# Moving the last two products of two layers behind the next layer's first product, with a matmul prelude on zeros and two conversions moved to DVE, in an attention and two-layer-pair kernel on one Trainium2 core

## The chip, the cores and the metric

The kernel runs on one core of one Trainium2 chip. The metric is device time in microseconds (us); a kernel is run several times and the median is given. The engines are PE (TensorE, matmuls), DVE (VectorE), ACT (ScalarE), POOL (GpSimd, here mostly an issuer of DMAs) and SP (SyncE, an issuer of DMAs). PSUM is the memory into which PE writes; here it is four tiles, ps0 to ps3, of two banks each, and a bank holds 448 columns of float32 results.

## The reference

Attention with a sigmoid in place of the softmax, then two pairs of dense layers; everything is float32:

```python
scores = (1 / 8) * q @ k.T - log(448)          # q, k, v: 4 batches, 12 heads, 448 x 64
x = sigmoid(scores) @ v                        # x: 1792 tokens x 768
h = x @ w_in;  g = h - tanh(h);  y = g @ w_out             # 768 -> 2048 -> 768
h = y @ w_in2; g = max(h, 0) + alpha * min(h, 0)           # 768 -> 2048
out = g @ w_out2                                           # 2048 -> 768
```

## The kernel before, in words

**Numbers.** A float32 operand is split into a high and a low float16 half. The high half is one scaled copy (ACT or DVE can do it), the low half is one instruction on DVE, which needs the high one. A product is three passes on PE (high by high, high by low, low by high; `PASSES`).

**Attention.** `scores` multiplies a pair of heads (`st0` to `st23`, the split of the loads `sqk0` to `sqk23`) into ps0, ps1 or ps2 in turn, ACT takes the sigmoid out of it, and `values` multiplies that by v into ps3. A ps tile is free for the next scores when its sigmoid is done. The first pair is loaded in two halves; every split is a node that either ACT or DVE may take ("AV").

**Layers.** The four dense layers are counted 0 to 3 in the code, and 0 and 2 are the wide ones (`layer_in`), 1 and 3 the narrow ones (`second_layer`, `fourth_layer`, both through `multiply_out`). Each layer multiplies 2 x 2 blocks with seven products instead of eight, in the order `SEQ` = 1, 2, 6, 5, 7, 4, 3; sums of blocks are formed on DVE or by accumulating DMAs. The tokens come in two halves (sb = 0, 1). In layers 0 and 2 each product of each quarter q is a node of 18 matmuls into a whole ps tile: products 1, 6, 7, 4 of a quarter go into ps0 or ps1 (by q % 2), 2 into ps2, 5 and 3 into ps3. After product 7 of a quarter ACT copies the tile out; product 4 then writes into the same tile. To hide that copy, products 4 and 3 of a quarter (`tail`) are emitted after products 1 and 2 of the next quarter. For the last quarter there is no next one, and they come right after product 7.

In layers 1 and 3 a product is twelve groups of six matmuls (four quarters of the contraction by three rows of blocks e = 0, 1, 2); a group takes one bank. Products 1, 6, 7, 4 accumulate in the three banks `YB`, products 2, 5, 3 in the three banks `ZB`. When the last quarter of product 1, 6, 7 or 4 is done, ACT reads the three `YB` banks (`copied`); `added` on DVE reads the `ZB` banks. Products 7 and 4 are neighbours and both write into `YB`.

**Order.** Nothing is issued in the order of the code. Every step is a node of `Plan` with costs and due times; PE's nodes keep the order in which they are added, and for ACT, DVE, POOL and SP the planner runs a clock of its own and takes whichever ready node is due first, so far as its tables (`AHEAD`, `CHAIN`, `KEEP_*`, `WIN_*`, `PACE`) let it. So the tables set what stands in each engine's queue, and an engine works its queue strictly in order. The planner keeps one entry for each bank; the tile framework underneath puts in the semaphore waits. The weights are put together from two words by DVE, split, stored to a scratch in device memory by POOL's DMAs and fetched back by SP's.

All instructions are recorded through one helper, so each has line L213 in the profile, and rows are told apart by operation, tile and time.

## Time and profile before

| | |
|---|---|
| median of 3 runs | 904.79 us (904.16 to 906.05) |
| the profiled execution's own time | 904.37 us |
| span in that profile, first to last instruction | 902.6 us |
| PE, DVE, ACT busy share of the span | 99%, 88%, 71% |
| granted TensorE clock over the span | 1.000 |

The profiled execution took 1.8 us more than its span. Times in rows count from the start of the span. Attention fills PE until 130 us; layer 0 then runs to 323, layer 1 to 515, layer 2 to 707 and layer 3 to 898. PE's busy time has modelled ends, so a busy PE can hide short stalls between matmuls.

### The profile page before, as it was taken

How to read it: one execution, taken by the hardware profiler on the slowest of the kernel's cores; microseconds unless marked ns; L12 is line 12 of the kernel's file. 1: busy time of each engine (PE TensorE's matmuls, PEld its weight loads, DVE VectorE, ACT ScalarE, POOL GpSimd, SP SyncE). 2: the span in 40 equal slices, each digit the busy share in tenths (PEclk: the TensorE clock that was granted, in tenths of full speed). 3: DMA queues.
4: the chain of work that ended last, by engine and by line, in shares of the span. 5: the costliest groups of instructions: out<-in, count | busy, mean ns of one | idle time of the engine just before them, and what ended most of it. 6: DMA issues, size and time to landing. Idle time of an engine off the chain costs nothing.

```text
span 902.6 us, 13531 instructions
## 1 busy us (share of the span) xinstructions
PE 889.6 (99%) x4992; PEld 436.9 (48%) x4992; DVE 794.3 (88%) x1002; ACT 637.6 (71%) x879; POOL 156.4 (17%) x243
## 2 busy tenths in 40 slices
PE   7999999999999999999999999999999999999998
PEld 2333335555555455555455555555555455555554
DVE  6999999999999999999999999999987998684310
ACT  7999998999999787998575766756564655332310
POOL 0122523341222110100123142112110000000000
PEclk9999999999999999999999999999999999999999
DMA  9999999999978975655599999679872445453431
GB/s 352 371 351 333 278 383 401 280 233 270 275 248 254 288 222 167 223 185 202 175 324 348 340 297 382 209 239 362 291 250 88 140 159 193 141 191 120 138 136 62
DMA packets 67490, 223.46 MB, mean 248 GB/s; under 512 B 8416, under 2 KB 14816, under 8 KB 67424
## 3 DMA queue, kind: packets, MB, share of 16 engines
q0 software_dynamic: 25664, 109.33, 38.3%
q1 hardware_dynamic: 41760, 113.27, 36.2%
q8 instruction: 39, 0.64, 0.3%
q14 instruction: 27, 0.22, 0.1%
HBM read 154.94 MB, written 49.55 MB: 227 GB/s over the span
## 4 chain that ended last, share of the span: by engine, by line
PE 87%; DVE 8%; ACT 2%; issue 2%; DMA 1%; POOL 0%; SPq 0%; DVEq 0%; ACTq 0%
PE ps L213 87%; DVE slot L213 8%; ACT slot L213 2%; DMA slot<-qk 1%; DVE sc L213 0%; POOL sc L213 0%; SPq L213 0%; POOL scr L213 0%; DVEq L213 0%; ACTq L213 0%
## 5 line engine op out<-in xcount | busy, mean ns | idle before, releaser
L213 PE MATMUL ps<-slot,slot 128*128 128x448 f16 (+2 forms) x4416 | 836.5, 370 | 4.1 <-ACT slot L213 2.4
L213 PEld LDWEIGHTS <-slot 128*128 128x128 f16 (+1 forms) x4608 | 416.8, 98 | 422.6 <-issue 32.8
L213 ACT ACTIVATE slot<-slot 128x896 f32<-128x896 f32 (+3 forms) x288 | 250.9, 903 | 72.6 <-DVE slot L213 54.9
L213 ACT ACTIVATE slot<-slot,sc 128x896 f16<-128x896 f32 (+2 forms) x170 | 169.9, 1020 | 95.7 <-PE ps L213 43.2
L213 DVE SCALAR_TENSOR_TENSOR slot<-slot,sc,slot 128x896 f16<-128x896 f32 (+1 forms) x160 | 174.9, 1115 | 34.6 <-ACT slot L213 34.4
L213 DVE TENSOR_TENSOR slot<-slot,slot 128x896 f32<-128x896 f32 (+2 forms) x178 | 177.2, 1018 | 0.2
L213 DVE SCALAR_TENSOR_TENSOR slot<-slot,slot 128x768 f16<-128x768 f32 (+2 forms) x137 | 131.4, 970 | 8.4 <-ACT slot L213 8.2
L213 POOL DMA_DIRECT2D scr<-slot x112 | 67.8, 605 | 352.8 <-DVE slot L213 318.8
L213 DVE SCALAR_TENSOR_TENSOR slot<-stage,slot 128x768 int32<-128x768 int32 x128 | 120.3, 955 | 0.2
L213 ACT ACTIVATE slot<-ps 128x448 f32<-128x448 f32 (+1 forms) x88 | 60.6, 709 | 32.9 <-PE ps L213 32.4
L213 ACT ACTIVATE slot<-ps,cst 128x896 f32<-128x896 f32 x84 | 80.2, 1027 | 2.1 <-PE ps L213 2.0
L213 DVE SCALAR_TENSOR_TENSOR slot<-ps,sc,slot 128x896 f32<-128x896 f32 (+1 forms) x42 | 39.5, 950 | 44.1 <-PE ps L213 31.3
L213 ACT ACTIVATE slot<-ps,sc 128x896 f32<-128x896 f32 (+1 forms) x56 | 46.8, 838 | 38.4 <-PE ps L213 38.2
L213 POOL DMA_DIRECT2D stage<-w x60 | 36.1, 602 | 181.3 <-DVE slot L213 152.9
L213 POOL DMA_DIRECT2D slot<-slot x56 | 52.2, 1018 | 61.0 <-DVE slot L213 33.2
L213 PE MATMUL ps<-slot 64*128 64x448 f16 (+1 forms) x576 | 57.6, 362 | 4.9 <-ACT slot L213 4.9
L213 DVE TENSOR_SCALAR slot<-stage 128x768 int32<-128x768 int32 x64 | 35.3, 557 | 6.8 <-PE ps L213 6.6
L213 PEld LDWEIGHTS ps<-slot,slot 128*64 128x64 f32 (+1 forms) x384 | 20.1, 135 | 38.6 <-issue 37.5
L213 DVE COPY_PREDICATED slot<-slot,slot 128x896 f32<-128x896 int32 x32 | 38.3, 1216 | 0.0
L213 DVE TENSOR_SCALAR slot<-slot 128x768 f16<-128x768 f32 (+2 forms) x50 | 28.9, 590 | 0.4 <-DMA slot<-qk 0.3
L213 ACT ACTIVATE junk<-slot 128x448 f16<-128x448 f32 (+1 forms) x36 | 25.4, 705 | 3.3 <-DVE slot L213 2.8
L213 DVE TENSOR_TENSOR slot<-ps,slot 128x896 f32<-128x896 f32 (+1 forms) x28 | 24.6, 889 | 2.2 <-ACT slot L213 1.3
(28 smaller groups left out, 141.9 us busy)
## 6 DMA issues: line engine op xcount, KB each, us to landing
slot<-scr SPq DMA_DIRECT2D x224, 384.0 KB, 4.6
stage<-w POOLq DMA_DIRECT2D x60, 768.0 KB, 7.4
scr<-slot POOLq DMA_DIRECT2D x112, 384.0 KB, 6.1
slot<-slot POOLq DMA_DIRECT2D x32, 384.0 KB, 7.0
slot<-qk SPq DMA_DIRECT2D x23, 448.0 KB, 7.9
slot<-v SPq DMA_DIRECT2D x12, 448.0 KB, 7.5
slot<-slot POOLq DMA_DIRECT2D x24, 224.0 KB, 7.9
out_t<-slot SPq DMA_DIRECT2D x24, 224.0 KB, 2.0
```

What stands on the lines that cost most here:

```text
L213: return lambda *args, **kw: self.tc.keep_in_program_order(f(*args, **kw))
```

## The change

The last two products of layers 0 and 2 are no longer emitted at the end of `layer_in` but handed to the next layer, which emits them behind its first product (sb = 0). For this the banks of layers 1 and 3 are dealt out anew: `YB` was one bank of each of ps0, ps1 and ps2 and is now both banks of ps0 and one of ps2; `ZB` was both banks of ps3 and one of ps2 and is now both banks of ps1 and one of ps2. DVE sets `junk` to zero and PE multiplies it nine times into ps3 before anything else. The high halves of `st1` and `st2` may go to DVE alone. The planner's tables get other numbers (two lines are shown), the costs of the attention nodes are a little lower, and the first six loads are taken to land a microsecond later.

```diff
-CHAIN = {0: 7, 1: 3, 2: 5, 3: 7}
+CHAIN = {0: 2, 1: 3, 2: 6, 3: 7}
...
-KEEP_W, KEEP_F, KEEP_P, WIN_F, WIN_O, WIN_P, SPARE_V, WIN_Q = 7, 5, 12, 14, 43, 29, 8, 16
+KEEP_W, KEEP_F, KEEP_P, WIN_F, WIN_O, WIN_P, SPARE_V, WIN_Q = 8, 8, 1, 14, 29, 8, 12, 24
+WARM = 9
...
-        add("AV", {"A": act(n, ptr=ptr), "V": vec(n, ptr, True)}, high, [*reads, *extra],
+        add(on, {"A": act(n, ptr=ptr), "V": vec(n, ptr, True)}, high, [*reads, *extra],
...
-                  (j,) if halves == 2 else (0, 1))
+                  (j,) if halves == 2 else (0, 1), on="V" if i in (1, 2) else "AV")
...
-    YB = ((0, 0), (1, 0), (2, 0))
-    ZB = ((3, 0), (3, 1), (2, 1))
+    YB = ((0, 0), (0, 1), (2, 0))
+    ZB = ((1, 0), (1, 1), (2, 1))
...
-    def multiply_out(m, sb, P, copied, added):
+    def multiply_out(m, sb, P, copied, added, between):
...
+            if pr == 1:
+                for each in between:
+                    each()
...
+    V.memset(junk, 0.0)
+    for _ in range(WARM):
+        PE.matmul(pst[3][:, 0, 0:S], junk[:, 0:128], junk[:, 0:S], start=True, stop=True)
...
                 tail = [fourth, third]
-        for each in tail:
-            each()
+        return tail
...
-    layer_in(0, copy_h, finish_h, last_h, ended_h)
+    tail = layer_in(0, copy_h, finish_h, last_h, ended_h)
     for sb in range(2):
-        second_layer(sb)
+        second_layer(sb, () if sb else tail)
```

Layers 2 and 3 are changed in the same way.

**Three places in the order of the instructions.** The first is DVE's queue from its first instruction, before; slot0 to slot7 hold the loads there, and the results are the splits of `st0` to `st4`.

```order
L213 SCALAR_TENSOR_TENSOR slot8_183<-slot0_175,slot8_183 128x448 [waits DMAHW0_49,Activation_49]
L213 SCALAR_TENSOR_TENSOR slot8_183<-slot0_175,slot8_183 128x448 [waits DMAHW1_49,Activation_49]
L213 SCALAR_TENSOR_TENSOR slot0_175<-slot1_176,slot0_175 128x896 [waits DMAHW2_49,DVE_49,Activation_49]
L213 TENSOR_SCALAR slot11_186<-slot2_177 128x896 [waits DMAHW3_49]
L213 SCALAR_TENSOR_TENSOR slot11_186<-slot2_177,slot11_186 128x896 [waits DVE_49]
```

And after the change (the helper's line is now L214):

```order
L214 MEMSET junk_235 128x448
L214 SCALAR_TENSOR_TENSOR slot10_185<-slot0_175,slot10_185 128x448 [waits DMAHW0_49,Activation_49]
L214 SCALAR_TENSOR_TENSOR slot10_185<-slot0_175,slot10_185 128x448 [waits DMAHW1_49,Activation_49]
L214 TENSOR_SCALAR slot11_186<-slot1_176 128x896 [waits DMAHW2_49]
L214 SCALAR_TENSOR_TENSOR slot11_186<-slot1_176,slot11_186 128x896 [waits DVE_49]
```

The memset is new and stands first. The high half of `st1` (TENSOR_SCALAR out of slot1) is now on DVE; before, ACT made it, and DVE's third instruction waited for ACT. In ACT's queue the sigmoids now follow the two half-width copies of `st0` directly.

The second place is PE's queue at the end of layer 0 (slot41, slot43 and slot47 are operands and weights). Before, product 7 of the last quarter, into ps1, is followed by product 4, into ps1 again:

```order
L213 LDWEIGHTS slot43_218
L213 MATMUL ps1_237<-slot41_216,slot43_218 128x448
L213 LDWEIGHTS slot47_222 [waits DMAHW0_49]
L213 MATMUL ps1_237<-slot29_204,slot47_222 128x448 [waits Activation_49]
L213 LDWEIGHTS slot47_222
```

After the change, product 7 is followed by layer 1's first group, into ps0:

```order
L214 LDWEIGHTS slot50_225
L214 MATMUL ps1_237<-slot5_180,slot50_225 128x448
L214 LDWEIGHTS slot47_222 [waits DMAHW0_49]
L214 MATMUL ps0_236<-slot3_178,slot47_222 128x448
L214 LDWEIGHTS slot47_222
```

The wait for ACT is gone there; product 4 into ps1, with its wait for ACT's copy, comes 72 matmuls later, and product 3 behind it.

The third place is ACT's queue in layer 1, sb = 0, around the copies after product 7. Before (the copies are the rows out of ps0, ps1 and ps2):

```order
L213 ACTIVATE slot34_209,mx_233<-slot44_219,sc_234 128x896 [waits DVE_49]
L213 ACTIVATE slot12_187<-ps0_236 128x448 [waits PE_49]
L213 ACTIVATE slot33_208<-ps1_237 128x448 [waits PE_49]
L213 ACTIVATE slot34_209<-slot47_222,cst_232 128x896 [waits Activation_49]
L213 ACTIVATE slot18_193<-ps2_238 128x448 [waits DMAHW5_49,PE_49]
```

After the change:

```order
L214 ACTIVATE slot14_189<-ps0_236 128x448 [waits DMAHW4_49,PE_49]
L214 ACTIVATE slot20_195<-slot18_193 128x896 [waits DVE_49]
L214 ACTIVATE slot12_187,mx_233<-slot1_176,sc_234 128x896 [waits DVE_49]
L214 ACTIVATE slot21_196,mx_233<-slot24_199,sc_234 128x896 [waits DVE_49]
L214 ACTIVATE slot12_187<-ps0_236 128x448 [waits PE_49,Activation_49]
L214 ACTIVATE slot16_191<-ps2_238 128x448 [waits DVE_49]
```

The first two copies now read two banks of one tile, ps0, and three activations of 896 columns stand between them, each of which waits for DVE.

## Rows read from the trace of the kernel before

**Rows 1.** PE's waits by releaser: us in total, times, longest us.

```profile
PE ps L213 <- ACT slot L213: 7.4, 5, 4.6
PE ps L213 <- DVE slot L213: 1.3, 2, 0.7
```

**Rows 2.** Stretches: length, busy time of PE, PEld, DVE, ACT, POOL, clock, DMA share.

```profile
20.00:130.00 110.00, 110.00 (x858) 36.94 (x856) 108.23 (x151) 107.78 (x144) 32.73 (x49) 1.00 0.98 341
130.00:320.00 190.00, 188.58 (x1002) 97.25 (x995) 186.96 (x234) 177.59 (x227) 52.42 (x75) 1.00 0.92 286
390.00:515.00 125.00, 124.21 (x657) 64.07 (x655) 123.69 (x158) 89.07 (x138) 25.24 (x38) 1.00 0.79 259
```

**Rows 3.** PE's timeline at the begin: start, length, count, idle before and its releaser.

```profile
5.35 2.44 PE L213 MATMUL ps<-slot 64*128 64x448 f16 x12
...
8.32 2.54 PE L213 MATMUL ps<-slot 64*128 64x448 f16 x18 [0.15 <-ACT slot L213]
11.02 0.76 PE L213 MATMUL ps<-slot 64*64 64x448 f16 x12 [0.15 <-ACT slot L213]
...
13.37 1.31 PE L213 MATMUL ps<-slot 64*128 64x448 f16 x12
```

**Rows 4.** ACT's timeline at the begin.

```profile
6.42 0.95 ACT L213 ACTIVATE slot<-slot 128x896 f16<-128x896 f32 x1 [1.85 <-DMA slot<-qk]
7.28 6.38 ACT L213 ACTIVATE slot<-ps,cst 128x896 f32<-128x896 f32 x7
```

**Rows 5.** DVE's timeline at the begin.

```profile
7.41 1.09 DVE L213 SCALAR_TENSOR_TENSOR slot<-slot,slot 128x896 f16<-128x896 f32 x1 [2.18 <-ACT slot L213]
8.42 0.62 DVE L213 TENSOR_SCALAR slot<-slot 128x896 f16<-128x896 f32 x1
```

**Rows 6.** PE's timeline, the four longest idle times after the begin.

```profile
315.95 2.24 PE L213 MATMUL ps<-slot,slot 128*128 128x448 f16 x11 [1.42 <-ACT slot L213]
...
354.33 1.86 PE L213 MATMUL ps<-slot,slot 128*128 128x448 f16 x9 [0.57 <-DVE slot L213]
...
449.25 2.05 PE L213 MATMUL ps<-slot,slot 128*128 128x448 f16 x10 [0.74 <-DVE slot L213]
...
700.32 1.86 PE L213 MATMUL ps<-slot,slot 128*128 128x448 f16 x9 [1.01 <-ACT slot L213]
```

**Rows 7.** ACT's timeline at the end of layer 0.

```profile
314.91 0.99 ACT L213 ACTIVATE slot<-ps,sc 128x896 f32<-128x896 f32 x1
```

**Rows 8.** DVE's timeline before two of those idle times end.

```profile
353.13 3.27 DVE L213 SCALAR_TENSOR_TENSOR slot<-slot,sc,slot 128x896 f16<-128x896 f32 x3
...
448.04 1.15 DVE L213 TENSOR_TENSOR slot<-ps,slot 128x448 f32<-128x448 f32 x2
```

**Rows 9.** ACT's timeline around the copies after product 7, layer 1, sb = 0.

```profile
390.46 0.94 ACT L213 ACTIVATE slot<-ps 128x448 f32<-128x448 f32 x2
391.31 1.03 ACT L213 ACTIVATE slot<-slot,cst 128x896 f32<-128x896 f32 x1
392.24 0.52 ACT L213 ACTIVATE slot<-ps 128x448 f32<-128x448 f32 x1
```

**Rows 10.** ACT's timeline before the same copies for sb = 1: two splits.

```profile
481.78 1.56 ACT L213 ACTIVATE slot<-slot 128x768 f16<-128x768 f32 x2
```

**Rows 11.** ACT's timeline around the same copies in layer 3, sb = 0.

```profile
773.43 0.63 ACT L213 ACTIVATE slot<-ps,sc 128x448 f32<-128x448 f32 x1 [6.98 <-PE ps L213]
773.96 1.03 ACT L213 ACTIVATE slot<-slot,sc 128x896 f16<-128x896 f32 x1
```

**Rows 12.** The page, part 5: groups with count, busy us, mean ns of one.

```profile
L213 PE MATMUL ps<-slot,slot 128*128 128x448 f16 (+2 forms) x4416 | 836.5, 370 | 4.1 <-ACT slot L213 2.4
...
L213 DVE COPY_PREDICATED slot<-slot,slot 128x896 f32<-128x896 int32 x32 | 38.3, 1216 | 0.0
```

**Rows 13.** The timeline's last rows of PE and DVE.

```profile
893.66 4.89 PE L213 MATMUL ps<-slot,slot 128*128 128x448 f16 x25
897.46 1.89 DVE L213 SCALAR_TENSOR_TENSOR slot<-ps,sc,slot 128x448 f32<-128x448 f32 x3 [24.75 <-PE ps L213]
```

24 lines of the change are left out of this document (12 added, 12 removed).

## The prediction

> **What bounds the kernel now.** I read the busy shares of the table first: PE 99% of the span, DVE 88%, ACT 71%. So a gain can only come out of PE's few stalls and out of the time before its queue is dense. PE's waits come to 7.4 us on ACT, 4.6 of it ahead of the first matmul, and 1.3 on DVE; none is put down to a DMA [rows 1]. The stretches say how much room the others have: from 20 to 130 us DVE is busy 108.23 and ACT 107.78 of 110, from 130 to 320 DVE 186.96 of 190, from 390 to 515 DVE 123.69 of 125 [rows 2]. PE is the bound, but DVE stands right behind it until layer 2; whatever lets PE run ahead by more than a few us there meets DVE.
>
> PE's timeline then shows where it stops. After the begin there are four stalls above 0.5 us: 1.42 and 1.01, released by ACT, and 0.57 and 0.74, released by DVE [rows 6]. The first two are the ends of layers 0 and 2: product 4 waits for ACT's copy of the tile that product 7 has just left. At the end of layer 0 that copy began at 314.91 and took 0.99 [rows 7].
>
> At the begin, twelve matmuls from 5.35 take 2.44 us, while twelve of the same shape from 13.37 take 1.31 [rows 3]. They run in pairs: six pairs at 0.37 apart against 0.19. 448 columns take 0.373 us at 1.2 GHz and 0.187 at 2.4, so the first scores ran at the lower of the clock's two levels, although the granted-clock column reads 1.00 everywhere [rows 2]. But what holds PE there is ACT: it idles 1.85 us for the second load, makes the high half of `st1` from 6.42 to 7.37, and only then begins seven sigmoids back to back at 7.28 [rows 4]; PE waits for a sigmoid at 8.32 and 11.02 [rows 3]. From 11.02 on its queue is dense.
>
> **The start.** The memset (448 columns; an estimate is no more than the 0.62 that DVE takes for 896 [rows 5]) and the nine matmuls (9 x 0.37 = 3.4 us at the lower level) fit before the first real matmul at 4.6 [rows 1]. The first score's third pair starts at 5.35 and ends 0.58 later even at the lower level, by 5.95 [rows 3], so the first sigmoid can begin 1.3 us earlier once the high half of `st1` is off ACT. At the higher level it could be 1.6 earlier; but on DVE that high half takes 0.62 from 6.42 (a TENSOR_SCALAR of this shape) and the low one 1.09 [rows 4, 5], to 8.15; the fourth score, with two pairs behind that and 0.35 for the last, ends about 8.75, when the fourth sigmoid is due (5.95 + 3 x 0.91 = 8.7). So the start gives **1.3** with either clock; range 0.8 to 1.6, since DVE gets 1.24 of work in a stretch in which it also has idle time [rows 5].
>
> **The tails.** Product 7 is now followed by layer 1's first product into ps0 and ps2, which PE left four products (some 13 us) or more earlier. The copies have 12 groups, 13.6 us, to finish. This takes away **1.42 + 1.01** [rows 6]. The new neighbour, product 2 into ps1 behind product 3, needs ps1 read out while product 3 runs (18 x 0.189 = 3.4 us [rows 12]): one copy of 0.99 in layer 0, two reads of that size in layer 2 [rows 7], which fit, so I cost it at nothing; were ACT 1 us late, that would be the price. The scales and splits of sb = 1 come 13.6 us later, but are due some 90 us later; DVE turns to weights meanwhile. In SP's queue the fetches of the two moved products change places with the four of layer 1's first product; PE waited for no fetch before [rows 1], so I cost that at nothing too.
>
> **DVE's stalls.** The 0.57 at 354 is a low half that DVE reaches too late, one of three in a row [rows 8]. In the new order about five instructions of some 1 us fewer stand ahead of it on DVE, so the stall goes, although PE comes 2.7 us (1.3 + 1.42) earlier. For the fourth quarter of that product there is only about one fewer; I put **0.3** (0 to 1.8) there, since DVE also has less idle time at the begin. The 0.74 at 449 is of another kind: PE wants bank 0 of ps2, and what ends the stall is DVE's second read from 448.04, out of bank 1 [rows 6, 8]. A wait is by tile, not by bank. The last rows say so again: the last three groups end at 898.55, 897.41 and 896.28 (1.135 each), and DVE, idle for 24.75, reads the first of them, in ps3, only at 897.46, when ps3's other bank is done too [rows 13]. In the new order that read of ps2 is emitted behind PE's group, the wait falls three groups later, and the **0.74** goes.
>
> **The price of pairing the banks.** This is what the new `YB` costs. Products 7 and 4 both write `YB`, and two of its banks are now one tile. With ps0, ps1, ps2 the copy of bank e had two groups' time, 2.27 us, before product 4 needed it. Now copy 0 cannot begin before group 1 of product 7 ends. Count from that end: product 4's first group is due at 0.97 (one group less the 0.17 by which a matmul's end overlaps the next [rows 12]), its second at 2.11. Four such places:
> - Layer 3, twice: copies of 0.53 apart and 0.63 long [rows 11], 0.05 to start, 0.06 to pass on: 1.27, so **0.3** each (0 to 0.8).
> - Layer 1, sb = 1: a weight split of 0.78 [rows 10] stands between the copies in the new order: 0.05 + 0.45 + 0.78 + 0.54 + 0.06 = 1.88, so **0.9** (0.3 to 1.5).
> - Layer 1, sb = 0: three activations of 896 columns at 0.93 stand between them (third place in the order): 0.05 + 0.45 + 2.79 + 0.52 + 0.06 = 3.87, against 2.11: 1.76. Two of the three wait for a predicated copy of 1.22 on a full DVE [rows 12], so I take **2.2**; between 0.6 (copy 1 has only to wait for product 4's first group) and 3.5 (both predicated copies late).
>
> Before, ACT had the first two in 0.94 [rows 9] and PE did not stop there.
>
> The Trainium skill speaks for the other result. "PSUM — Partial Sum Buffer", section "PSUM bank collisions raise a hardware error", says that engines collide by bank and quadrant of partitions, and advises to guard by bank; by that rule two banks of one tile need no wait, the four places would cost nothing, and the net gain would be 5.04 - 0.3 = 4.7 us. By the rows the wait is there all the same, put in by tile: the rule bears on what the chip needs, not on the waits that this program has.
>
> **The sum.** Gains 1.3 + 1.42 + 1.01 + 0.57 + 0.74 = 5.04. Losses 0.3 + 0.3 + 0.3 + 0.9 + 2.2 = 4.0. Net 1.0 us: 904.37 - 1.0 = 903.3 for an execution like the profiled one (its span and the 1.8 around it, which I leave as they are). The median of the runs lies 0.42 above that execution, so I forecast **903.7**. A measurement of this kernel can tell about 0.2% from no change, which is 1.8 us; this forecast is inside.
>
> **Rivals.**
> - *The pairing is cheap* (0.33). ACT and DVE are ahead of PE at the four places and the copies cost only what they must: 0.6 + 0.3 + 0 + 0, and the net gain is 5.04 - 0.3 - 0.9 = 3.8: 904.8 - 3.8 = 901.0. For it: ACT is busy only 89 of 125 us from 390 on [rows 2]. Against it: the three activations stand in the queue between the copies, and an engine does not pass them. The skill's rule above, were the waits by bank, would end here too.
> - *The paired copies are late by ACT and DVE both: slower* (0.12). The place is the same four passages. The copy after product 7 already began late in layer 1 before, at 390.46 [rows 9]. If such a delay of 1 us meets each passage, and the three activations wait for DVE in full, the four cost 3.5 + 1.9 + 2 x 1.3 = 8.0 instead of 3.7, and the time is 908.0. It decides, that is passes 906.6, from 6.6 us of stalls there on.
> - *The early gains are not kept* (0.07). ACT and DVE are 98% busy from 20 to 130 [rows 2]; if they cannot run 1.3 us earlier, or DVE cannot follow PE in layer 1 (the 0.57 stays, the fourth quarter costs 1.8), the gain comes back as stalls: 903.7 + 1.3 = 905.0 without the start, 903.7 + 0.57 + 1.5 = 905.8 with DVE late in layer 1.
> - *The forecast* (0.48): 903.7, own range 902.4 to 905.2; about a tenth of it lies below 903.
>
> The range that should hold 8 in 10 reaches from the cheap pairing, with 0.4 for a begin that gives 1.6, to the early gains lost with a little of the late copies: 900.6 to 906.2. Faster by over 0.2% (below 903.0): 0.33 and 0.05 of the forecast's own, 0.38. Slower by over 0.2% (above 906.6): 0.12. Within: 0.50.
>
> **What would show it.** Right: the seven sigmoids from about 6.0; no stall at the ends of layers 0 and 2; in layer 1, a PE stall near 2 us about 386 us (product 4's second group, released by ACT) and one near 0.9 about 485; 0.3 twice in layer 3, all before groups into ps0. Wrong: PE passing these places without a stall, or stalls released by DVE or a DMA anywhere in layers 1 to 3 that together pass 2 us; PE stalling on ACT within attention; or sigmoids that still begin after 7 us.

## The result

The changed kernel is **slower**: 909.90 us median of six runs (908.53 to 912.83) against 905.42 (904.16 to 906.72) for the kernel before; ratio 1.0051, 95% interval 1.0037 to 1.0065. That is 4.5 us more, where 1.7 less was forecast, and outside the range of the forecast. The profiled execution took 908.66 us with a span of 906.9, against 904.37 and 902.6, so the two profiles differ by the 4.3 us that are to be explained. Of the changed kernel's six runs the two with a mean granted clock of 1.000 took 908.53 and 908.66 (the profiled one) and the four with 0.998 or 0.996 took 909.58 to 912.83, so its median also holds time at the lower clock, of which its profile shows nothing.

I begin with PE's milestones, found by counting matmuls in both timelines; the last column says how far the changed kernel is behind.

| PE begins | before | after | behind |
|---|---|---|---|
| the seventh scores (twelve 64x64 matmuls) | 11.02 | 11.64 | 0.62 |
| layer 0 | 130.48 | 132.07 | 1.59 |
| layer 1, sb = 0, product 2 | 336.37 | 336.38 | 0.01 |
| the same, product 6, fourth quarter | 360.94 | 361.83 | 0.89 |
| layer 1, sb = 1 | 418.83 | 422.34 | 3.51 |
| layer 2 | 515.28 | 519.35 | 4.07 |
| the last matmul's end | 898.55 | 902.48 | 3.93 |

So between these two profiles the start lost where it should have gained (how much of that is a load that landed later stands under "The begin" below); the moved products gave back all of that at the end of layer 0; and layer 1 lost more than 3 us after that. PE's waits of the changed kernel, by releaser (us in total, times, longest), and the group of layer matmuls on its page, whose last numbers are the idle time ahead of them, answer to [rows 1, 12]:

```profile
PE ps L214 <- ACT slot L214: 5.2, 6, 2.0
PE ps L214 <- DVE slot L214: 3.0, 5, 1.5
PE ps L214 <- DVE junk L214: 1.4, 1, 1.4
```

```profile
L214 PE MATMUL ps<-slot,slot 128*128 128x448 f16 (+2 forms) x4416 | 837.2, 370 | 6.6 <-ACT slot L214 4.3 <-DVE slot L214 2.0
```

The idle time ahead of that group rose from 4.1 to 6.6. Here 0.89 of it stands in attention and 5.65 in the four layers (before 4.0). PE's timeline, the longer of these stalls, each the idle time at the row's end (compare [rows 6]):

```profile
33.88 1.72 PE L214 MATMUL ps<-slot,slot 128*64 128x448 f32 x8 [0.89 <-ACT slot L214]
...
353.89 40.00 PE L214 MATMUL ps<-slot,slot 128*128 128x448 f16 x210 [1.45 <-DVE slot L214]
395.85 14.92 PE L214 MATMUL ps<-slot,slot 128*128 128x448 f16 x78 [1.96 <-ACT slot L214]
410.99 9.24 PE L214 MATMUL ps<-slot,slot 128*128 128x448 f16 x48 [0.23 <-ACT slot L214]
...
491.38 19.46 PE L214 MATMUL ps<-slot,slot 128*128 128x448 f16 x102 [0.66 <-ACT slot L214]
511.41 2.81 PE L214 MATMUL ps<-slot,slot 128*128 128x448 f16 x14 [0.57 <-ACT slot L214]
...
781.29 3.00 PE L214 MATMUL ps<-slot,slot 128*128 128x448 f16 x15 [0.28 <-DVE slot L214]
...
877.35 25.13 PE L214 MATMUL ps<-slot,slot 128*128 128x448 f16 x132 [0.28 <-DVE slot L214]
```

All four old stalls of [rows 6] are gone and ten are new; two of 0.11 (778.58 and 874.63) are not shown. A stall costs PE about 0.17 more than its idle time, since the overlap of two matmuls is lost with it: at product 2's begin (336.38) the 1.42 that went had made up 1.58.

The begin, first PE's timeline, to be read against [rows 3]:

```profile
1.38 3.54 PE L214 MATMUL ps<-junk 128*128 128x448 f16 x9 [1.38 <-DVE junk L214]
4.85 2.68 PE L214 MATMUL ps<-slot 64*128 64x448 f16 x18
7.77 0.36 PE L214 MATMUL ps<-slot 64*128 64x448 f16 x2 [0.24 <-DVE slot L214]
8.89 1.84 PE L214 MATMUL ps<-slot 64*128 64x448 f16 x16 [0.76 <-DVE slot L214]
11.64 0.76 PE L214 MATMUL ps<-slot 64*64 64x448 f16 x12 [0.92 <-ACT slot L214]
```

and ACT's and DVE's, against [rows 4, 5]:

```profile
6.19 1.91 ACT L214 ACTIVATE slot<-ps,cst 128x896 f32<-128x896 f32 x2 [1.65 <-PE ps L214]
8.93 1.01 ACT L214 ACTIVATE slot<-ps,cst 128x896 f32<-128x896 f32 x1 [0.83 <-issue]
10.59 3.70 ACT L214 ACTIVATE slot<-ps,cst 128x896 f32<-128x896 f32 x4 [0.65 <-DVE slot L214]
```

```profile
7.09 0.63 DVE L214 TENSOR_SCALAR slot<-slot 128x896 f16<-128x896 f32 x1 [1.89 <-DMA slot<-qk]
7.75 1.09 DVE L214 SCALAR_TENSOR_TENSOR slot<-slot,slot 128x896 f16<-128x896 f32 x1
8.76 0.62 DVE L214 TENSOR_SCALAR slot<-slot 128x896 f16<-128x896 f32 x1
9.41 1.09 DVE L214 SCALAR_TENSOR_TENSOR slot<-slot,slot 128x896 f16<-128x896 f32 x1
```

The first sigmoid does begin 1.09 us earlier (6.19, before 7.28). But the seven are no longer in one piece: the third begins at 8.93, right behind the end of a low half on DVE (7.75 + 1.09 = 8.84), the fourth at 10.59, right behind the next (9.41 + 1.09 = 10.50). The slots say why: the planner gave sigmoids 3 and 4 the slots of `sqk1` and `sqk2`, the loads that those low halves read last (and sigmoid 7 that of `sqk3`). In the old plan the seven sigmoids ran in one piece [rows 4]; here an order of reuse sets their time.

Stretches (length, busy time of PE, PEld, DVE, ACT, POOL, clock, DMA share, GB/s); the first two cut the begin, the others are those of [rows 2]:

```profile
2.00:20.00 18.00, 16.09 (x108) 5.80 (x110) 13.02 (x17) 11.76 (x15) 0.00 (x0) 1.00 0.99 386
20.00:38.00 18.00, 17.11 (x140) 5.67 (x132) 14.54 (x19) 15.86 (x22) 3.34 (x6) 1.00 1.02 410
20.00:130.00 110.00, 109.11 (x852) 36.53 (x846) 105.00 (x145) 105.12 (x141) 33.01 (x50) 1.00 1.00 345
130.00:320.00 190.00, 190.00 (x1010) 97.68 (x1007) 187.34 (x236) 173.72 (x223) 50.77 (x74) 1.00 0.88 274
390.00:515.00 125.00, 121.58 (x641) 62.44 (x639) 122.43 (x155) 87.66 (x138) 24.34 (x37) 1.00 0.78 249
```

From 2 to 38 us the DMA engines have a share of about 1, and neither ACT nor DVE is full. The share alone does not single this stretch out (it is 1.00 from 20 to 130 as well); that ACT idles for loads does. Its timeline ahead of the stall at 33.88 shows how that reaches PE: it idles for a load, splits `sqk9`, and only then copies the tile (ps3) that PE waits for.

```profile
32.01 0.95 ACT L214 ACTIVATE slot<-slot 128x896 f16<-128x896 f32 x1 [0.59 <-DMA slot<-qk]
32.87 0.96 ACT L214 ACTIVATE slot<-ps 128x448 f32<-128x448 f32 x2
```

The largest stalls are both in layer 1, sb = 0. DVE's timeline ahead of 353.89:

```profile
349.10 0.60 DVE L214 TENSOR_TENSOR slot<-ps,slot 128x448 f32<-128x448 f32 x1
349.64 1.07 DVE L214 TENSOR_TENSOR slot<-slot,slot 128x896 f32<-128x896 f32 x1
350.64 1.13 DVE L214 SCALAR_TENSOR_TENSOR slot<-slot,sc,slot 128x896 f16<-128x896 f32 x1
351.70 1.07 DVE L214 TENSOR_TENSOR slot<-slot,slot 128x896 f32<-128x896 f32 x1
352.70 1.14 DVE L214 TENSOR_TENSOR slot<-ps,slot 128x448 f32<-128x448 f32 x2
```

DVE reads a bank with the first row, does three other things, and reads two more with the last; the second of those is ps2's bank 1, and PE, which only wants bank 0, resumes behind it. ACT's timeline ahead of 395.85, which answers to [rows 9]:

```profile
391.96 0.52 ACT L214 ACTIVATE slot<-ps 128x448 f32<-128x448 f32 x1
392.39 0.94 ACT L214 ACTIVATE slot<-slot 128x896 f32<-128x896 f32 x1
393.23 1.03 ACT L214 ACTIVATE slot<-slot,sc 128x896 f32<-128x896 f32 x1
...
394.25 1.03 ACT L214 ACTIVATE slot<-slot,sc 128x896 f32<-128x896 f32 x1
...
395.28 0.95 ACT L214 ACTIVATE slot<-ps 128x448 f32<-128x448 f32 x2
```

This is the forecast's picture: three activations between the two copies out of ps0, and PE's second group waits. The end, DVE's last reads against [rows 13]: again it idles long and reads a bank only when the tile's other bank is done (the tile is now ps1, where the new `ZB` has its two banks).

```profile
901.38 1.89 DVE L214 SCALAR_TENSOR_TENSOR slot<-ps,sc,slot 128x448 f32<-128x448 f32 x3 [10.35 <-PE ps L214]
```

### The profile page after: what moved, and what is told of

The parts are those of the page before. It is cut to its first block, busy times and chain, and to the rows that moved or that the text cites. A ratio compares the mean times of both kernels' runs of the same rounds, so it can differ in the third digit from the quotient of the medians.

```text
span 906.9 us, 13565 instructions
## 1 busy us (share of the span) xinstructions
PE 892.6 (98%) x5001; PEld 437.4 (48%) x5001; DVE 798.9 (88%) x1007; ACT 628.5 (69%) x875; POOL 155.4 (17%) x243
## 4 chain that ended last, share of the span: by engine, by line
PE 86%; ACT 4%; DMA 4%; DVE 3%; issue 2%; SPq 0%; POOL 0%; ACTq 0%; DVEq 0%
PE ps L214 86%; ACT slot L214 4%; DVE slot L214 3%; DMA slot<-qk 2%; DMA scr<-slot 1%; DMA stage<-w 1%; SPq L214 0%; POOL slot L214 0%; ACT junk L214 0%; ACTq L214 0%; DVEq L214 0%
## 5 line engine op out<-in xcount | busy, mean ns | idle before, releaser
L214 PE MATMUL ps<-slot,slot 128*128 128x448 f16 (+2 forms) x4416 | 837.2, 370 | 6.6 <-ACT slot L214 4.3
L214 PEld LDWEIGHTS <-slot 128*128 128x128 f16 (+1 forms) x4608 | 416.1, 98 | 422.2 <-issue 34.9
L214 ACT ACTIVATE slot<-slot 128x896 f32<-128x896 f32 (+4 forms) x295 | 256.9, 904 | 58.2 <-DVE slot L214 43.4
L214 ACT ACTIVATE slot<-slot,sc 128x896 f16<-128x896 f32 (+2 forms) x164 | 163.5, 1020 | 93.4 <-PE ps L214 56.5
L214 DVE SCALAR_TENSOR_TENSOR slot<-slot,sc,slot 128x896 f16<-128x896 f32 (+1 forms) x160 | 175.0, 1111 | 53.2 <-ACT slot L214 53.0
L214 DVE TENSOR_TENSOR slot<-slot,slot 128x896 f32<-128x896 f32 (+2 forms) x178 | 176.1, 1014 | 0.6 <-ACT slot L214 0.4
L214 DVE SCALAR_TENSOR_TENSOR slot<-slot,slot 128x768 f16<-128x768 f32 (+2 forms) x137 | 131.5, 969 | 7.7 <-ACT slot L214 6.4
L214 POOL DMA_DIRECT2D scr<-slot x112 | 67.0, 599 | 344.0 <-DVE slot L214 305.3
L214 DVE SCALAR_TENSOR_TENSOR slot<-stage,slot 128x768 int32<-128x768 int32 x128 | 120.6, 952 | 0.2
L214 ACT ACTIVATE slot<-ps 128x448 f32<-128x448 f32 (+1 forms) x88 | 60.6, 712 | 50.1 <-PE ps L214 47.6
L214 ACT ACTIVATE slot<-ps,cst 128x896 f32<-128x896 f32 x84 | 80.6, 1045 | 4.9 <-PE ps L214 3.2
L214 ACT ACTIVATE slot<-ps,sc 128x896 f32<-128x896 f32 (+1 forms) x56 | 46.2, 839 | 48.0 <-PE ps L214 47.7
L214 POOL DMA_DIRECT2D slot<-slot x56 | 50.7, 945 | 88.8 <-DVE slot L214 71.3
L214 POOL DMA_DIRECT2D stage<-w x60 | 35.8, 605 | 142.2 <-DVE slot L214 139.7
L214 DVE SCALAR_TENSOR_TENSOR slot<-ps,sc,slot 128x896 f32<-128x896 f32 (+1 forms) x42 | 39.3, 948 | 22.8 <-PE ps L214 13.3
L214 PE MATMUL ps<-slot 64*128 64x448 f16 (+1 forms) x576 | 56.4, 356 | 1.9 <-DVE slot L214 1.0
L214 DVE TENSOR_SCALAR slot<-stage 128x768 int32<-128x768 int32 x64 | 35.1, 556 | 5.7 <-PE ps L214 5.0
L214 PEld LDWEIGHTS ps<-slot,slot 128*64 128x64 f32 (+1 forms) x384 | 20.1, 135 | 39.5 <-issue 35.6
L214 DVE COPY_PREDICATED slot<-slot,slot 128x896 f32<-128x896 int32 x32 | 38.2, 1211 | 0.0
L214 DVE TENSOR_SCALAR slot<-slot 128x896 f16<-128x896 f32 (+2 forms) x48 | 28.6, 602 | 3.9 <-DMA slot<-qk 2.1
L214 ACT ACTIVATE junk<-slot 128x448 f16<-128x448 f32 (+1 forms) x36 | 25.5, 707 | 4.9 <-DVE slot L214 4.5
L214 DVE TENSOR_TENSOR slot<-ps,slot 128x896 f32<-128x896 f32 (+1 forms) x28 | 24.4, 884 | 2.3 <-ACT slot L214 1.8
```

Of the source, the lines that this page charges most:

```text
L214: return lambda *args, **kw: self.tc.keep_in_program_order(f(*args, **kw))
```

## The experiments

Ratios are against runs of the kernel before, taken on the same chip along with each experiment (its medians: 905.15 to 906.11). All compute the whole of the reference. Where instructions change places, the planner's finished list is edited before it is emitted:

```diff
-            if not dry:
-                n.emit(e)
             log.append((now, e, n))
...
+        def at(k, e, *names):
+            return [i for i, x in enumerate(log) if x[1] == e and set(names) <= set(x[2].touched)][k]
+
+        for what, behind in MOVES:
+            x = log.pop(at(*what))
+            log.insert(at(*behind) + 1, x)
         self.log = log
+        for now, e, n in log:
+            n.emit(e)
```

and a result gets a slot of its own by `self.slots[OWN[name]] if name in OWN else self.where[name][1]`.

### The begin

*No zeros.*

```diff
-WARM = 9
...
-    V.memset(junk, 0.0)
-    for _ in range(WARM):
-        PE.matmul(pst[3][:, 0, 0:S], junk[:, 0:128], junk[:, 0:S], start=True, stop=True)
```

> The changed kernel without the memset and the nine matmuls on zeros; every queue is otherwise word for word the same. My theory: the zeros only hasten the first scores, while the third and fourth sigmoid wait for DVE (their output slots are those of the loads sqk1 and sqk2). So the first sigmoid begins 0.3 to 0.7 us later than 6.19, the third still at about 8.9, PE's seventh scores still at about 11.6, and the time stays at 909.9 within 0.5. Rival A, the zeros disturb the loads (sqk1 landed 0.7 later than before): it lands near 6.3 again, the seventh scores begin near 10.9, time about 909.2. Rival B, the zeros are worth what I forecast: the seventh scores begin 1 us later, time about 910.9.

909.03 us, ratio 1.0037 (1.0025 to 1.0049). The seventh scores begin at 11.62 (with zeros 11.64). The zeros are worth nothing. `sqk1` landed at 7.03 here, so it was not the zeros that held it up (rival A).

*The high halves back on ACT, or slots of their own for three sigmoids.*

```diff
-            if e == "V":
+            if e == "V" and dst not in ("st1", "st2"):
```

> The changed kernel with the high halves of st1 and st2 back on ACT, at the same places of the plan's order. My theory: the first sigmoid begins behind the high half of st1, near 8.0 instead of 6.19, another 0.95 stands between the first and second, the seventh scores begin near 12.6 instead of 11.64, and the time is 0.5 to 1.5 longer, 910.4 to 911.4. Rival, the move to DVE is itself what lost the time at the begin: the seventh scores begin near 11.0 and the time is 0.6 shorter, 909.3.

```diff
+OWN = {"sa0,2": 48, "sa0,3": 49, "sa0,6": 50}
```

> The changed kernel with three sigmoids of the first group (the third, fourth and seventh) written into slots that nothing has used yet, in place of the slots of sqk1, sqk2 and sqk3; the order of every queue is the same. My theory: the third sigmoid begins near 8.1 instead of 8.93 and the fourth near 9.5 instead of 10.59, the seventh scores near 10.6 instead of 11.64; the lead of 1.0 is kept into attention, the stall of 0.9 near 33 us shrinks, and the time is 1 to 2 shorter, 907.9 to 908.9. Rival, attention is bound by ACT and DVE and gives the lead back: the stalls from 15 to 130 us grow by what the begin gains, time 909.9.

On ACT: 910.21, ratio 1.0048 (1.0033 to 1.0063); the seventh scores begin 0.8 later, at 12.46, there is no stall at 33 us, and layer 0 begins at 131.93, level. With own slots: 911.02, ratio 1.0055 (1.0037 to 1.0072). The seventh scores begin at 10.31, 1.33 earlier (1.10 of it when counted from the landing of `sqk1`, see the table below), so the slots were what held the sigmoids; but PE's timeline pays it back, and more, and the stretch behind the stall is at half the clock:

```profile
35.57 3.25 PE L214 MATMUL ps<-slot,slot 128*64 128x448 f32 x8 [3.42 <-ACT slot L214]
```

```profile
36.00:39.00 3.00, 3.00 (x10) 0.61 (x8) 3.00 (x5) 3.00 (x5) 0.55 (x1) 0.51 0.70 233
```

Layer 0 begins at 135.37. My time for this run was wrong; the rival, a lead given back, was nearer (it said 909.9).

*Splits that wait for loads moved behind sigmoids and copies, without and with own slots.*

```diff
+MOVES = [((0, "A", "sqk8"), (0, "A", "sa2,3")), ((0, "V", "sqk8"), (2, "V", "#stage0")),
+         ((0, "A", "sqk9"), (0, "A", "sa2,5")), ((0, "V", "sqk9"), (0, "V", "sqk10"))]
+OWN = {"sa2,5": 47}
```

> The changed kernel with the splits of st8 and st9 some five instructions later in ACT's and DVE's queues (behind the sigmoids that they stood ahead of). In the changed kernel and in three variants of it PE went on after the stall near 33 us 1.97 after the load sqk9 had landed (31.91, 32.46, 33.60). My theory: ACT waits for these two loads with PE's sigmoids and copies queued behind it, so the stall goes wherever the loads land up to 33, the time is 1.0 to 1.6 shorter, 908.3 to 908.9, and the runs lie closer together. Rival, the loads hold up PE by another way (DVE's low halves, the next loads): a stall of like size before 45 us, time 909.9.

> The kernel with the later splits of st8 and st9, and the third, fourth and seventh sigmoid in slots of their own. My theory: with the wait for the loads off ACT's queue the lead of 1.3 from the begin (seventh scores at 10.3 in place of 11.64) lasts to the end of attention, and the time is 1.0 to 1.4 below that of the kernel with the later splits alone, 907.0 to 907.8. Rival, attention is bound by ACT and DVE or by the loads: PE gives the lead back in stalls before 130 us and the time equals that of the later splits alone.

909.47, ratio 1.0044 (1.0026 to 1.0061), and 911.18, ratio 1.0060 (1.0043 to 1.0078). The first loses the stall at 33 and gets one of 0.47 at 64.49. The second begins the seventh scores at 10.03 and then stalls 0.67, 0.84, 0.58 and 1.09 before 67 us; layer 0 begins at 133.57, against 131.81 without own slots. PE that begins this early gets nothing for it. That it is the loads alone is not shown: in the second run DVE is busy without a break from 38 to 70 us, where three of the four stalls lie, and ACT, which releases them, waits for DVE there (1.08 up to 39.20, 0.79 up to 64.49); its stretches show it:

```profile
38.00:50.00 12.00, 10.42 (x79) 3.55 (x80) 12.00 (x17) 9.69 (x14) 2.16 (x4) 1.00 0.88 313
50.00:70.00 20.00, 18.91 (x150) 6.27 (x148) 20.00 (x27) 18.72 (x27) 3.76 (x7) 1.00 0.92 330
```

*Twice the zeros.*

```diff
-WARM = 9
+WARM = 18
```

> The changed kernel with eighteen matmuls on zeros in place of nine, so that the first scores begin 1.7 to 3.4 us later. In the runs so far PE came to the scores of st9 between 48.0 and 49.3 wherever the seventh scores had begun (11.1 to 12.5). My theory, the loads hold PE there, so a begin that is later by up to 2 us costs nothing: st9 at 49.0 to 49.6 and the time within 0.7 of 909.9. Rival, the begin counts in full: 911.5 or more.

909.55, ratio 1.0047 (1.0035 to 1.0059). The first real matmul begins at 7.78 instead of 4.85, the seventh scores at 12.31, and against the changed kernel it costs nothing: it has no stall at 33 us, and layer 0 begins at 131.78.

*The landing of the second load.* Over the profiles of all runs `sqk1` landed anywhere from 5.84 to 7.82 us, though SP issued it at 1.63 or 1.64 in each. Counted from that landing, the begins are steady:

| begin | `sqk1` lands | seventh scores begin | time between |
|---|---|---|---|
| before (3 profiles) | 5.84, 6.34, 7.52 | 10.52, 11.02, 12.20 | 4.68 |
| changed (11 profiles) | 6.48 to 7.82 | 11.06 to 12.40 | 4.58 or 4.59 |
| without zeros | 7.03 | 11.62 | 4.59 |
| 18 zeros | 7.00 | 12.31 | 5.31 |
| high halves on ACT | 7.01 | 12.46 | 5.45 |
| own slots (2 profiles) | 6.55, 6.83 | 10.03, 10.31 | 3.48 |

(In a twelfth profile with the changed begin the next load, `sqk2`, came late too, at 9.34, and the time is 5.19.) So at an equal landing the changed begin gains 0.10, and own slots would have given 1.20, close to the 1.3 of the forecast. The 0.62 lost in the table of milestones is a landing later by 0.72, less that 0.10. Three profiles of the old begin are too few to say whether the change itself makes the load land later.

The stall at 33 us differs between executions as well: of the eleven profiles with the changed begin and unaltered splits of `st8` and `st9`, six have none, three have 0.18 to 0.30, and two 0.89 and 1.15. Where PE does not stall between the seventh scores and layer 0 (11 of the 20 profiles, with either begin), layer 0 begins 119.46 after the seventh scores. So a late begin is passed on in full where nothing stops PE, and the early begin of own slots was lost to stalls both times.

### The places in layers 1 and 3

*Old banks for sb = 1 alone.*

```diff
+OLD = {(0, 1): (1, 0), (1, 0): (3, 0), (1, 1): (3, 1)}
-    def bank(k):
+    def bank(k, sb):
+        k = OLD.get(k, k) if sb else k
...
```

> The changed kernel with the banks of the kernel before in layers 1 and 3 for sb = 1 alone (YB one bank each of ps0, ps1, ps2; ZB both of ps3 and one of ps2); the order of every queue is the same. My theory, two banks of YB in one tile make the stalls: those of 0.66 at 491, and of 0.11 and 0.28 at 875 and 877, go, and the time is 1.0 to 1.6 shorter, 908.3 to 908.9; the 0.57 at 511 stays, since ps2 is shared as it was. Rival, ACT is late there by itself, whatever the banks: the stalls stay within 0.3 of what they were, time 909.9.

907.13, ratio 1.0016 (1.0004 to 1.0027): 2.8 us below the changed kernel. The stalls at 491, 511 and in layer 3's second half are gone. PE's timeline runs through the place:

```profile
478.76 41.40 PE L215 MATMUL ps<-slot,slot 128*128 128x448 f16 x218
```

That the 511 went too I had not expected. Not all of the 2.8 belongs to the banks: this profile has no stall at 33 us either (changed kernel 0.89), and its sb = 0 half is otherwise stalled as before (1.44, 1.97, 0.23).

*The two copies behind product 7 brought together.*

```diff
+MOVES = [((0, "A", "sy4,0", "ps0"), (0, "A", "sy3,0", "ps0")), ...]
+OWN = {"sy4,0": 47}
```

> The changed kernel with ACT's second copy out of ps0 after product 7 of layer 1 directly behind the first one (sb = 0: ahead of the three activations of 896 columns, into a slot of its own; sb = 1: ahead of a split of 768). PE, DVE, POOL and SP keep their order. My theory: the stall at 396 is these three activations between two copies out of one tile, so it falls from 1.96 to 0.1 to 0.4, that at 491 from 0.66 to 0.1 to 0.3, and the time is 2.0 to 2.4 shorter, 907.5 to 907.9. Rival, DVE's predicated copies set the pace there: PE stalls at the next group instead, and the time stays within 0.5 of 909.9.

908.90, ratio 1.0042 (1.0026 to 1.0058). The 1.96 falls to 0.21, but the third copy, now behind the three activations, costs 0.89 at 396.37, and the 0.23 at 411 becomes 0.94. The three activations are the cost, whichever copy stands behind them: the rival in its place, but the time lies between my theory (907.5 to 907.9) and the rival (909.4 to 910.4).

*Reads of ps2 put behind PE's group into its other bank.*

```diff
+MOVES = [((0, "V", "sy2,0", "ps2"), (0, "T", "sV1,6,1,0", "ps0")), ((0, "A", "sy2,0", "junk"), (0, "V", "sy2,0", "ps2")),
+         ((1, "A", "sy5,0", "ps2"), (0, "T", "sV1,3,0,0", "ps2")), ((1, "A", "sy5,1", "ps2"), (0, "T", "sV1,3,1,1", "ps2"))]
```

> The changed kernel with three reads of ps2 recorded behind PE's next group into the other bank of ps2, in place of ahead of it: DVE's read at 353, ACT's at 410 and at 511. The wait is by tile, so the group no longer waits for the read, and the read waits for the group. My theory: the stalls of 1.45, 0.23 and 0.57 go, the time is 2.5 to 2.8 shorter, 907.1 to 907.5. Rival, DVE and ACT are behind PE there anyway: the stalls come back one to three groups later and the time stays at 909.9 within 0.5.

910.45, ratio 1.0051 (1.0033 to 1.0069). The stalls at 353, 410 and 511 are gone, so a read of the other bank did cause them. PE's timeline a little later:

```profile
361.47 0.35 PE L221 MATMUL ps<-slot,slot 128*128 128x448 f16 x1 [0.21 <-ACT slot L221]
363.21 2.05 PE L221 MATMUL ps<-slot,slot 128*128 128x448 f16 x10 [1.40 <-DVE slot L221]
```

One of 1.34 at 457.81 comes in sb = 1. The wait moved; the rival again.

*Four high halves moved from DVE to ACT, so that DVE has slack ahead of 353.*

```diff
+ON_ACT = ("st:(1, 3, 2)", "st:(1, 7, 2)", "sQ2,2,0", "st:(1, 6, 3)")
-            if e == "V":
+            if e == "V" and dst not in ON_ACT:
```

> The changed kernel with four high halves that DVE made between 290 and 339 us (2.4 us of its work) made by ACT, at the same places of the plan's order; ACT idles 22 us between 260 and 366. In the runs so far PE's fourth quarter of product 6 in layer 1 (361.8 in the changed kernel) began at 347.1 plus DVE's idle time up to there, within 0.3, wherever PE stood at the begin. My theory, DVE sets PE's time there: the stall of 1.45 at 354 falls below 0.4 and the time is 1.2 to 1.8 shorter, 908.1 to 908.7. Rival, the stall is that of the shared ps2 alone, whatever DVE has to do: it stays, time 909.9.

910.02, ratio 1.0044 (1.0029 to 1.0058). By then I held that DVE's load set PE's time throughout layer 1, because PE's stalls always added up to DVE's time. PE's timeline refutes it:

```profile
353.84 6.40 PE L215 MATMUL ps<-slot,slot 128*128 128x448 f16 x33 [1.44 <-DVE slot L215]
```

DVE now idles for 0.13 ahead of the read at 349.03, and the stall is as long as with a full DVE (1.45). That my sums had come out was bookkeeping: DVE itself waits for PE's group at 349, and what it then does in order, some 4.7 us, is what PE waits for.

### The parts by themselves

*Moved products back at the end of their layers, with new banks and with old.*

```diff
-        return tail
+        for each in tail:
+            each()
+        return ()
```

> The changed kernel with the last two products of layers 0 and 2 emitted at the end of the layer again; new banks, tables and begin stay, the planner orders the rest anew. My theory, up to product 6 of layer 1 DVE sets PE's time: the stall at the end of layer 0 (about 1.4) comes back, but the one at 354 shrinks by as much and PE is at product 6 where it was within 0.5; only the stall of 1.0 at the end of layer 2 is lost, time 910.5 to 911.3. Rival, both tails are gains of their own: time 2.4 longer, 912.3.

> The changed kernel with old banks and the last two products at the end of their layer: new tables, zeros and high halves on DVE alone. My theory: these alone are about even with the kernel before (the begin gives nothing, since PE is held by the loads until 49 us anyway; the tables were made for other banks): 905.0 to 907.5, and against the same kernel with new banks (910.5) the banks cost 3 to 5. Rival, tables and begin are what made the changed kernel slow: 908.5 or more.

*The kernel before with the moved products and the new banks, and with the new banks alone.*

> The kernel before with the moved products and the new banks alone: its own tables, no zeros, high halves as they were. My theory: layer 0's tail gives nothing lasting (DVE), layer 2's gives 1.0, the paired and shared banks cost 3 to 5 us in layers 1 and 3, so it is slower than before by 2 to 4 us: 907.4 to 909.4 where the kernel before has 905.4. Rival, the new tables and the begin made the changed kernel slow, and the moved products are the gain that I forecast: 904.0 to 905.0.

> The kernel before with the new banks of layers 1 and 3 and nothing else; the planner orders the rest anew. My theory: two of the banks that ACT reads after product 7 are now one tile, and its copies stand where the planner put them without knowing that, so stalls before groups into ps0 come to 3 to 6 us and the time is 3 to 6 longer than before, 908.5 to 911.5. Rival, the pairing is cheap by itself and the moved products made the version with both slow: 905.4 to 906.5.

| run | median | ratio (95%) |
|---|---|---|
| new tables, new banks, products not moved | 910.46 | 1.0046 (1.0029 to 1.0064) |
| new tables, old banks, products not moved | 905.74 | 1.0001 (0.9992 to 1.0009) |
| old tables, new banks, products moved | 913.93 | 1.0086 (1.0066 to 1.0107) |
| old tables, new banks, products not moved | 906.89 | 1.0011 (1.0001 to 1.0020) |

The stalls of 1.22 and 1.0 at the layers' ends come back in the first, but the 1.45 and the 1.96 go, and others come (1.15 at 375.35, 0.83 and 0.96 later); the net is 0.6 above the changed kernel, so that is all that the moved products are worth under this plan. The second row says that tables, zeros and high halves together are worth nothing measurable. The third is slower than I expected. Its largest stalls are 2.34 at 404.06, behind the first matmul of a group and released by DVE, which speaks for an operand and not for a bank, and 1.76 and 1.36 at the begin of layer 1's sb = 1, with one matmul between. The fourth cost 1.0 where I expected 3 to 6. So, with the planner ordering the rest anew each time, the banks cost 4.7 us by the medians (4.1 by the ratios) under the new tables and 1.0 under the old, and moving the products gave 0.6 under the new and cost some 7 under the old: they have no price of their own, only one in an order.

### Mending

*Old banks in sb = 1, copies together, high halves on ACT.* (Own slots for `sy4,0` and `sy5,0` in this and the next three, in the third of the four for `sQ4,1,0` as well.)

```diff
+OLD = {(0, 1): (1, 0), (1, 0): (3, 0), (1, 1): (3, 1)}
...
+MOVES = [((0, "A", "sy4,0", "ps0"), (0, "A", "sy3,0", "ps0")), ((0, "A", "sy5,0", "ps2"), (0, "T", "sV1,7,3,0", "ps2")),
+         ((1, "A", "sy5,0", "ps2"), (0, "T", "sV1,3,0,0", "ps2"))]
```

> The changed kernel with the four high halves on ACT, the old banks for sb = 1, and for sb = 0 of layer 1 all three copies after product 7 ahead of the activations that wait for DVE, and the read of ps2 at 410 behind PE's group. My theory: the stalls at 354, 396, 411, 491, 511, 875 and 877 go or fall below 0.4 each; from 909.9 the time falls by 1.5 for DVE, 2.3 for the banks and 1.5 for the copies, to 904.1 to 905.5. Rival, DVE and ACT give most of it back one group later, as with the copies together alone: 906.5 to 907.5.

905.93, ratio 1.0004 (0.9994 to 1.0014). The copies' places in sb = 0 are mended (0.21 is left), but the read at 353 is not, in spite of the high halves (1.44 at 353.81), and a stall of 1.30 at 422.77 is new: sb = 1's first group into ps1 waits for DVE's read of sb = 0, since two layouts of the banks meet there.

*One bank only back in sb = 1, and the read at 353 moved; high halves on DVE again.*

```diff
+OLD = {(0, 1): (3, 0)}
+MOVES = [..., ((0, "V", "sy2,0", "ps2"), (0, "V", "sQ6,1,0"))]
```

> The changed kernel with: for sb = 1 the second bank of YB in ps3, so that no two of YB share a tile; for sb = 0 of layer 1 all three copies after product 7 ahead of the activations that wait for DVE; DVE's read of ps2 at 353 two places earlier, and ACT's at 410 behind PE's group. High halves stay on DVE. My theory, which bank shares a tile and where its reads stand in the queue is what layers 1 and 3 lost: the stalls at 354, 396, 411, 491, 511, 875 and 877 go or fall below 0.4, none of that size comes in their place, and from 909.9 the time falls by 1.5, 2.3, 0.4 and 2.3, to 902.8 to 904.3, below both kernels. Rival, ACT and DVE are behind PE there and other stalls come in their place, as in the version with the banks of before for sb = 1: 905.0 to 907.0.

905.23, ratio 1.0005 (0.9993 to 1.0016). All places that its theory names are at 0.22 or less; 0.99 (360.66), 0.67 (425.31) and 0.31 (453.02) are left, and in layer 3 the 0.28 before sb = 0's group into ps2 (777.49). The time missed the theory (902.8 to 904.3): the rival's range has it.

*These three as well, and product 7's groups into ps2 put last; then once more, milder.*

```diff
+MOVES = [..., ((1, "V", "sy2,0", "ps2"), (1, "V", "sy0,0", "ps1")), ((0, "V", "sy2,1", "ps2"), (0, "V", "sQ6,2,1")),
+         ((0, "T", "sV1,7,2,0", "ps2"), (1, "T", "sV1,7,3,0", "ps0")), ...]
```

> The version with banks and order mended, and five moves more: DVE's reads of ps2 at 425 and 453 earlier in its queue, a sum of DVE and an activation of ACT behind the split that PE waits for at 359, and in product 7 of layers 1 and 3 (sb = 0) the third quarter's group of ps2 behind the fourth quarter's two groups of ps0, so that their copies have two groups' time. My theory: the stalls of 0.99, 0.22, 0.67, 0.31, 0.11 and 0.28 fall to 0.5 us together, the time is 2 to 3.5 us below that version, 901.7 to 903.2, and below the kernel before. Rival, ACT and DVE are the limit and other stalls take their place: 904.5 to 905.5.

906.97, ratio 1.0022 (1.0008 to 1.0036): my own moves made a stall of 2.15 at 451 and one of 0.69 at 421, and the new order of groups gave nothing. ACT's timeline tells why:

```profile
777.02 1.16 ACT L222 ACTIVATE slot<-ps,sc 128x448 f32<-128x448 f32 x2 [5.96 <-PE ps L222]
```

The last group into ps0 had ended at 775.85, but the copy out of it begins behind the next group, into ps2 (end 776.99): in the trace PE raises its semaphore at 777.00 and not at 775.85.

```diff
+MOVES = [..., ((1, "V", "sy2,0", "ps2"), (0, "T", "sV1,1,0,1", "ps2")), ((0, "V", "sy2,1", "ps2"), (0, "T", "sV1,6,0,1", "ps2")),
+         ((0, "V", "sG0,1,0,0", "sG0,0,0,0"), (0, "V", "sQ6,3,0")), ((1, "A", "sG1,0,1,1"), (0, "A", "sQ6,3,0"))]
```

> The version with banks and order mended (905.2) and four moves more: DVE's reads of ps2 at 425 and 453 right behind PE's first group into ps2 of that product, ahead of other work in DVE's queue, and ahead of PE's fourth quarter of product 6 (359) the split before a sum on DVE and before an activation on ACT. My theory: the stalls of 0.99, 0.67 and 0.31 fall below 0.4 together, the time is 1.5 to 2.5 below that version, 902.7 to 903.7, and 1.5 to 3 below the kernel before. Rival, DVE sets PE's time and other stalls take their place: 904.5 to 905.9.

**903.77 us against 906.11, ratio 0.9983 (0.9974 to 0.9992): faster than both kernels.** PE's waits and the group of layer matmuls:

```profile
PE ps L222 <- ACT slot L222: 2.3, 4, 0.9
PE ps L222 <- DVE slot L222: 1.6, 3, 0.8
```

```profile
L222 PE MATMUL ps<-slot,slot 128*128 128x448 f16 (+2 forms) x4416 | 836.8, 370 | 1.6 <-DVE slot L222 0.9 <-ACT slot L222 0.5
```

Idle time ahead of them is 1.6 (before 4.1, changed kernel 6.6). From layer 0's begin to the last matmul's end this profile is 2.2 us shorter than that of before. So the change with one bank dealt back, two results in slots of their own and eight instructions in another place is worth some 2 us, in the best of four such kernels.

## Why the prediction was wrong

It put the kernel within 0.2% of before and gave "slower" 0.12. Of the signs of being wrong that it named, two came: PE stalled on ACT within attention (0.89), and stalls released by DVE in layers 1 to 3 just pass 2 us together (1.45, 0.28, 0.28). Of its steps:

- **The start (gain 1.3; in the two profiles a loss of 0.6, 1.6 by layer 0).** Two steps failed. "The fourth score ends about 8.75, when the fourth sigmoid is due" followed the sigmoid's input, not the slot it writes into; at an equal landing of `sqk1` the seventh scores gained 0.10, and with own slots 1.20, which shows that cause. And "none is put down to a DMA" was true of PE and was taken for all engines, although the DMA share of 0.98 stood in the same rows [rows 2]: `sqk1` landed 0.72 later than in the profile of before, and the stall of 0.89 stands behind the landing of `sqk9`. Both differ between executions of one code, so the 1.6 lost by layer 0 belongs to these two profiles and is not shown to be a cost of the change; with old banks and products not moved the same begin and tables cost nothing measurable (ratio 1.0001, at most 0.8 us by the interval). An earlier begin was not kept: earlier by 1.3 and 1.6 gave 911.0 and 911.2, later by 0.7 and 0.8 gave 909.6 and 910.2. The low clock of the first scores was read rightly, and the nine zeros did shorten them, for nothing. Why the own-slot runs are not merely level but slower by about 1 us is shown only as far as the stalls go.
- **The tails (1.42 + 1.01): right for the two stalls, not for the time.** Both are gone, and PE is level with before at 336.38; but with the products back at the layers' ends the time rose by only 0.6, since other stalls went.
- **"The stall goes" (0.57) and "the 0.74 goes": right for those two, wrong as a sum.** I had the rule for a read of a shared tile and applied it to the old stalls alone. At 353 (sb = 0) the order is the mirror image of that at 449: the read of ps2's bank 1 is emitted ahead of PE's group into bank 0, and PE waits 1.45. Moving that read took the stall away, though other stalls came in its place; lightening DVE did not (1.44). The bank-wise guard that the Trainium skill advises ("PSUM — Partial Sum Buffer", section "PSUM bank collisions raise a hardware error") would know no such wait; the trace has it, by tile.
- **The fourth quarter (0.3): none** at its place.
- **Pairing (3.7): right in place and size, in the largest with some luck.** Forecast 2.2, 0.9, 0.3, 0.3; idle 1.96, 0.66, 0.11, 0.11, which with 0.17 for each overlap lost is 3.5. The 2.2 put 0.4 down to predicated copies on a full DVE; ACT did not idle between the three activations, but its first copy began 0.34 behind the end of PE's group (391.96 and 391.62), because another activation stood ahead of it. Old banks in sb = 1 took away the 0.66 and a 0.11, copies brought together cut the 1.96 to 0.21.
- **No term at all: ps2 shared by `YB` and `ZB` at four more places,** 0.23, 0.57, 0.28 and 0.28, with the overlaps some 2.0. The prediction counted only the copies out of ps0. The sharing is as old as the kernel before; with old banks in sb = 1 the 0.57 and one of the 0.28 went although ps2 stayed shared, so there it takes the pairing as well.

From the forecast of -1.0 to the +4.3 measured there are 5.3: the start 2.9 (1.2 the slots, 0.7 the landing of `sqk1`, 1.0 mostly the stall behind `sqk9`), the read at 353 1.6, the four others 2.0 and the end 0.4 (behind the last matmul, not explained), less 0.7 for the overlaps that the four old stalls had cost too, 0.3 for the fourth quarter and 0.2 for the pairing: 5.7, closed to within 0.4. The rival on the slower side had the sign and not the cause: its four passages cost 3.5, not 8.0. The one on lost early gains came true in the effect of its first half, with a weight of 0.07; its cause, a full ACT and DVE, was not what held the sigmoids.

What stays open: how much of the median's 4.5 is the begin (the two profiles alone put 1.6 there, the run with old banks nothing) and how much the lower clock of four of the six runs; what the moved products would do with the old banks, which was not run; and why the banks cost 4.7 us under one set of tables and 1.0 under the other, which is known place by place, not as a rule.

## What to carry to other kernels

Before pricing a faster begin, read the DMA share of that stretch and look for engines that idle for a load: where they do, ask when the loads land, and count each milestone from the landing ahead of it, in more than one profile, before calling it a gain or a loss. When two accumulators share a tile, list every read of either and look where it stands against the group into the other, in both halves of a loop, and not only at the stalls that the old profile has. An edit of tiles and an edit of order have no separate prices: here the same banks cost 1.0 or 4.7 us, and one bank dealt back, two results in slots of their own and eight instructions in another place turned 4.5 us of loss into 2.3 of gain.

## What the hardware showed beside

**A stall of 2 us may be followed by the lower clock, or not.** The changed kernel and the one with 18 zeros both stall at the same place, 1.96 and 1.97 us. The granted clock behind it, in the changed kernel and then the other (the number behind POOL's; 1.00 is the level of 2.4 GHz, 0.50 that of 1.2):

```profile
396.00:399.00 3.00, 3.00 (x17) 1.56 (x16) 2.76 (x6) 3.00 (x5) 0.00 (x0) 1.00 0.41 143
399.00:402.00 3.00, 3.00 (x18) 1.56 (x16) 3.00 (x5) 3.00 (x4) 0.00 (x0) 1.00 0.36 124
```

```profile
396.00:399.00 3.00, 3.00 (x11) 1.27 (x10) 1.83 (x3) 2.52 (x3) 0.00 (x0) 0.56 0.47 155
399.00:402.00 3.00, 3.00 (x16) 1.43 (x14) 2.51 (x4) 2.58 (x3) 0.00 (x0) 0.87 0.31 113
```

27 matmuls instead of 35 in six microseconds; from this place to the stall at 491 or 492 the second took 1.4 us more (96.96, against 95.53). Of the ten profiles with a stall of 1.96 or 1.97 only that of the 18 zeros has the lower clock behind it. The lower clock also followed stalls of 3.42 (0.51 from 36 to 39) and 2.15 (0.57 from 451 to 455), and in the kernel with old tables, new banks and moved products it came with 1.76 and 1.36 in a row (0.50 from 424 to 427.4), but not behind 2.34 (1.00 from 404 to 408). The changed kernel's runs spread with it: 908.5 at a mean clock of 1.0, 912.8 at 0.996; where in those runs the clock fell is not recorded. So a stall near 2 us can cost more than its length, a reason to split it.

**Loads land up to two microseconds apart between executions:** `sqk1`, the third load that SP issues, was there at 6.34 in the profile of before and at 7.06 in that of the changed kernel, with the same issues ahead of it, and from 5.84 to 7.82 over all profiles.

**A reader waits for the signal that the program gives:** the copy at 777.02 above began with the end of the group behind its own, where PE's semaphore rose; this is this program's choice and no limit of the chip that a run here shows.
